# Spreading the reciprocal of `den` over the head dimension: from a round trip through DRAM to row-tiled TensorE products

## The chip, the cores and the metric

The kernel runs on one core of one Trainium2 chip. The metric is the device time of that core in microseconds (us); of several runs the median is taken.

## The reference, cut to what matters

The output is a sum of three parts, all from one layer-normalized input `xn` of 2048 tokens by 640 features: the input itself, a linear attention with 32 heads of 20 features (part A), and an update of the 8 tokens with the largest router score (part B).

```python
q, k, v = qkv[0], qkv[1], qkv[2]                     # 32 heads, Dh = 20
phi = lambda t: jnp.where(t > 0, t + 1, jnp.exp(t)) + 1e-6
pq, pk = phi(q), phi(k)
kv = jnp.einsum("bhsd,bhse->bhde", pk, v)
z = jnp.einsum("bhsd->bhd", pk)
num = jnp.einsum("bhqd,bhde->bhqe", pq, kv)
den = jnp.einsum("bhqd,bhd->bhq", pq, z)[..., None] + 1e-6
o = num / den
...                                                  # A = o @ wo
...                                                  # B = xn + update of 8 tokens
return x + _A_ref(xn, A_wqkv, A_wo) + _B_ref(xn, ...)
```

What the change touches is `num / den`. `den` has one value for each head and token; the kernel scales `pq` by `1/den` ahead of the last product, so each of these values is needed 20 times, once for each feature of its head.

## The kernel before, in words

Tokens lie in 16 tiles of 128. The order on each engine is the order in which the program issues its instructions; semaphores follow from which instruction reads and writes what.

1. A loop over the 16 tiles normalizes (VectorE `norm_dve`, with the reciprocal root by GpSimd `root_pool`, lines 186 and 187), transposes `xn` by DMA into `xnT` (`tr_dma`, SyncE, line 229), makes `k` (`k_half`, line 237) and `phi(k)` (`k_phi`), part of `q` (`q_mm`, line 274), and accumulates `xn` transposed times `pk` (`g1`, line 266). SyncE loads the weights of part B in pieces in between; the last weights (`wv`, `wo`, rest of `wu`, and `wd` by `load_wd`, line 131) are issued behind the loop.
2. A middle stage picks the 8 tokens, forms `kv` and multiplies it with `wo` into `Ms` (`kv_mm` line 617, `m_unit` line 634), runs the gated layer of part B (`gate_up`, line 717) and the rest of `q`. `pqT` holds `phi(q)` with features on partitions and tokens along the free axis.
3. `den_mm` (line 568) makes `den` with products tiled by columns: four chunks of tokens land on four groups of 32 partitions (32 heads each). `den_act` (lines 577 and 578) makes the reciprocal `rden` by Ln and Exp on ScalarE. This happens three times: for tokens 0 to 1023, 1024 to 1535 and 1536 to 2047.
4. `rden` has heads on partitions, and `pqT` has features on partitions. The spreading from one to the other goes through DRAM: `rden_out` or `rden_out_b` (line 595) writes each head's row 20 times into a DRAM tile, and `rden_in` or `rden_in_b` (line 601) reads it back into a part of `spare` with features on partitions. VectorE then multiplies `pqT` with it, 256 tokens at a time (`rden_mul`, line 605) and from tile 8 on 128 at a time (`rden_mul_b`, line 609). `sprb[0]` holds the spread values of tiles 8 to 11 and `sprb[1]` those of 12 to 15.
5. The last loop runs over the tiles, one `t` each: `o_mm` (line 782) makes ten products with `Ms` into two PSUM banks, banks 0 and 1 for even and 2 and 3 for odd `t`; `o_out` (line 791) adds `x` on VectorE and issues the store of the tile (line 796). At `t == 0` the loop holds the `down` products of part B (line 727), `den_mm` and `den_act` of the last 512 tokens, their way through DRAM (issues alternating between ScalarE and SyncE), and the scaling of the 8 updated rows `y8` on ScalarE (line 833), which GpSimd then adds by an indirect DMA to a DRAM copy of the late rows (`s_dram`, line 837). At `t == 5` ScalarE loads those rows back into `x_sb` (line 842). `rden_mul_b(t + 2)` stands behind `o_out(t)` for `t` from 6 to 13, so tile 12 is scaled behind `o_out(10)`. `o_last` (lines 803 to 821) does tile 15.

Of the kernel before, what the change touches and what calls it, by code (L numbers as in the profile page):

```python
# [8 lines left out]
P = 128  # L9
S = 2048  # L10
D = 640
H = 32
DH = D // H
F = 1536
T = S // P
KC = D // P
FC = F // P
# [12 lines left out]
BF16 = mybir.dt.bfloat16  # L30
# [4 lines left out]
ALU = mybir.AluOpType  # L35
# [3 lines left out]
def kernel(  # L39
# [12 lines left out]
    nc = tc.nc  # L52
    V, A, G, PE = nc.vector, nc.scalar, nc.gpsimd, nc.tensor
# [12 lines left out]
    def sb(name, shape, dtype=BF16):  # L66
        return sm.tile(shape, dtype, tag=name, name=name)

    ps = psum.tile([P, 8, 512], F32, tag="ps", name="ps")
    rd = tc.dram_tile([4, D, 256], BF16, name="rd")  # L70
    rdb = [tc.dram_tile([D, 512], BF16, name=f"rd{tb}") for tb in (2, 3)]
    s_dram = tc.dram_tile([S - NS, D], BF16, name="s_dram")

    x_sb = big.tile([P, T, D], BF16, tag="x_sb", name="x_sb")
# [9 lines left out]
    wu = big.tile([P, KC, F], BF16, tag="wu", name="wu")  # L84
# [3 lines left out]
    SP = nc.sync  # L88
# [20 lines left out]
    def kcw(w, src, lo, hi):  # L109
        SP.dma_start(w[:, lo:hi, :], src.rearrange("(kc p) n -> p kc n", p=P)[:, lo:hi, :])  # L110
# [19 lines left out]
    def load_wd(lo, hi):  # L130
        SP.dma_start(wd[:, lo:hi, :], B_w_down.rearrange("(fc p) n -> p fc n", p=P)[:, lo:hi, :])
# [42 lines left out]
    def stat(t, b):  # L174
        V.bn_stats(out=stats[:, t, b, :], in_=x_sb[:, t, b * HW : (b + 1) * HW])  # L175
        if b:
            V.bn_aggr(out=mv[:, t, :], in_=stats[:, t, :, :])  # L177

    def root_act(t):
        sl = slice(t, t + 1)  # L180
        A.activation(lg[:, sl], mv[:, t, 1:2], AF.Ln, bias=eps5[:])
        A.activation(rs[:, sl], lg[:, sl], AF.Exp, scale=-0.5)

    def root_pool(t, n=1):
        sl = slice(t, t + n)
        G.tensor_scalar_add(t2[:, sl], mv[:, sl, 1], EPS_BF16)  # L186
        G.tensor_tensor(out=rs[:, sl], in0=t2[:, sl], in1=mhalf[:, 0:n], op=ALU.pow)  # L187

    def shift(t, n):
        sl = slice(t, t + n)  # L190
        V.scalar_tensor_tensor(
            out=nm[:, sl], in0=mv[:, sl, 0], scalar=-1.0, in1=rs[:, sl], op0=ALU.mult, op1=ALU.mult
        )

    def norm_dve(t):
        V.tensor_scalar(  # L196
            out=xn[:, t, :], in0=x_sb[:, t, :], scalar1=mv[:, t, 0:1], scalar2=rs[:, t : t + 1],
            op0=ALU.subtract, op1=ALU.mult,
        )
# [28 lines left out]
    def tr_dma(t):  # L228
        nc.sync.dma_start_transpose(xnT[:, :, t * P : (t + 1) * P], xn[:, t, :])
# [3 lines left out]
    def k_half(t, b):  # L233
        b0 = K_BANK.get(t, 0)
        n = HW + (b if t else 0)
        for kc in range(KC):
            PE.matmul(  # L237
                ps[:, b0 + b, 0:n],
                lhsT=xnT[:, kc, t * P : (t + 1) * P],
                rhs=wk[:, kc, b * HW : b * HW + n],  # L240
                start=(kc == 0), stop=(kc == KC - 1),
            )
# [68 lines left out]
    def const_mask():  # L311
# [11 lines left out]
            G.tensor_copy(mask[:, b, :], m4[:, 4 * b : 4 * b + HB])  # L323
        return mask

    cst = {}

    def const_small():
# [120 lines left out]
    def adds(t, n):  # L449
        G.tensor_scalar_add(rs1[:, t : t + n], rs[:, t : t + n], 1.0)  # L450
        for i in range(t, t + n):
            add_s(i)
# [5 lines left out]
    for t in range(5, T):  # L458
        n = t + 4
        if 9 < n <= T:  # L460
            norm_dve(n - 1)
            tr_dma(n - 1)
            if pieces and n < T:
                kcw(*pieces.pop(0))
            shift(n - 1, 1)
        halves = (1, 0) if t == 5 else (0, 1)
        for b in halves:
            k_half(t, b)
        if n < T:
            if t == 5:  # L470
                stat(n, 0)
            stat(n, 1)
            root_pool(n)
        if n + 1 < T:
            stat(n + 1, 0)
        k_act(t, halves)
        if t == 5:
            root_act(8)
            norm_dve(8)
            tr_dma(8)  # L480
            kcw(*pieces.pop(0))
            k_phi(4)
            q_phi(2)
        if t in q_at:
            q_mm(q_at[t])
            q_act(q_at[t])
        if t > 5:
            g1(t - 4)
        k_phi(t)
        if t in q_at:  # L490
            q_phi(q_at[t])
        if t == 5:
            shift(0, 9)
        if t in add_at:
            adds(*add_at[t])

# [10 lines left out]
    load_cols(wv, 0, KC, 2 * D)  # L507
    load_wo()
    kcw(wu, B_w_up, 2, 3)
    kcw(wu, B_w_up, 3, KC)  # L510
    for i in range(0, FC, 4):
        load_wd(i, i + 4)
    PE.transpose(psb[0:T, 1, 0:P], r_all[:], ident[:])
    g1(T - 4)
    r_row = sb("r_row", [T, P], F32)
# [7 lines left out]
    for i, src in enumerate((cand, idxu)):  # L523
        V.tensor_tensor(
            out=candm[:, i, :, :], in0=src[:].unsqueeze(1).to_broadcast([T, T, C]), in1=sel_b,
# [7 lines left out]
        start=True, stop=True,  # L533
# [15 lines left out]
        out=junk[:, 0:C], in0=posf[:], scalar=1.0, in1=cst["sel8"][:], op0=ALU.mult, op1=ALU.mult,  # L549
# [3 lines left out]
        out=junk[:], in0=cst["iof"][:, 0:P], scalar=cols[:, 0:1], in1=allc[:, 1, :],  # L553
# [20 lines left out]
    def den_act(o, w, bank):  # L574
        ld = sm.tile([P, w], F32, tag="ld", name=f"ld{o}")
        rden = sb(f"rden{o}", [P, w])
        A.activation(ld[:], ps[:, bank, 0:w], AF.Ln, bias=cst["eps6"][:])
        A.activation(rden[:], ld[:], AF.Exp, scale=-1.0)
        return rden
# [14 lines left out]
    def rden_out_b(eng, i, rden, j):  # L594
        eng.dma_start(  # L595
            rdb[i][:, j * P : (j + 1) * P].rearrange("(h i) t -> h i t", i=DH),
            rden[32 * j : 32 * j + 32, :].unsqueeze(1).to_broadcast([32, DH, P]),
        )

    def rden_in_b(i):  # L600
        SP.dma_start(sprb[i], rdb[i][:, :].rearrange("(m p) t -> p m t", p=P))
# [5 lines left out]
    def rden_mul_b(t):  # L607
        sl = pqT[:, :, t * P : (t + 1) * P]
        V.tensor_tensor(  # L609
            out=sl, in0=sl, in1=sprb[t // 12][:, :, t % 4 * P : (t % 4 + 1) * P], op=ALU.mult  # L610
        )

    def kv_mm(bs, bank):
# [29 lines left out]
    for t in range(T):  # L643
        cols4 = pk[:, t, :].rearrange("p (m j f) -> p m j f", j=4, f=32)
        for j in range(4):
            PE.matmul(
                ps[32 * j : 32 * j + 32, 7, 0 : KC * 32].rearrange("p (m f) -> p m f", f=32),
                lhsT=cst["ones"][:], rhs=cols4[:, :, j, :],
                start=(t == 0), stop=(t == T - 1), tile_position=(0, 32 * j),
# [10 lines left out]
        out=junk[:, 0:C], in0=gv[:], scalar=1.0, in1=cst["sel8"][:], op0=ALU.mult, op1=ALU.mult,  # L660
# [8 lines left out]
        out=gate[:, 1:2], in0=gate[:, 0:1], scalar1=1e30, scalar2=1.0, op0=ALU.min, op1=ALU.add  # L669
# [6 lines left out]
        out=gate[:, 0:1], in0=cols[:, 1:2], scalar1=float(NS), scalar2=float(2 * S),  # L676
# [3 lines left out]
        out=gate[:, 1:2], in0=cols[:, 1:2], scalar=-float(NS), in1=gate[:, 0:1],  # L680
# [4 lines left out]
    for t in range(13, T):  # L685
        V.tensor_scalar(
            out=x_sb[:, t, :], in0=x_sb[:, t, :], scalar1=rs1[:, t : t + 1],
# [14 lines left out]
    sprb = [sp_rows(8, 12, 512), sp_rows(12, T, 512)]  # L702
# [21 lines left out]
    def down():  # L724
# [22 lines left out]
        out=eg[:, 1, :], in0=eg[:, 0, :], scalar1=1e30, scalar2=1.0, op0=ALU.min, op1=ALU.add  # L747
# [40 lines left out]
    def o_out(t):  # L788
        b0 = 2 * (t % 2)
        o_t = evk.tile([P, 2, HW], BF16, tag=("ek", "rk")[t % 2], name=f"o{t}")  # L790
        V.tensor_tensor(  # L791
            out=o_t[:], in0=ps[:, b0 : b0 + 2, 0:HW],
            in1=x_sb[:, t, :].rearrange("p (b f) -> p b f", b=2), op=ALU.add,
        )
        eng = nc.sync if t % 2 == 0 and t > 2 else nc.scalar
        eng.dma_start(out_v[:, t, :], o_t[:].rearrange("p b f -> p (b f)"))

    def o_last(t):
# [24 lines left out]
    for t in range(T - 1):  # L823
        o_mm(t)
        if t == 0:
            down()
            den_mm(1536, P, 6)
            rden3 = den_act(1536, P, 6)
            for j in range(4):
                rden_out_b((A, SP)[j % 2], 1, rden3, j)  # L830
            rden_in_b(1)
            for i in range(4):
                A.activation(  # L833
                    y8[:, i * QW : (i + 1) * QW], ps[32 * i : 32 * i + C, 5 + 2 * (i % 2), 0:QW],
                    AF.Identity, scale=gate[32 * i : 32 * i + C, 2:3],
                )
            G.indirect_dma_start(  # L837
                s_dram[:, :], bass.IndirectOffsetOnAxis(ap=idx_i[0:C, 1:2], axis=0), y8[:], None,
                bounds_check=S - NS - 1, oob_is_err=False, compute_op=ALU.add,
            )  # L840
        if t == 5:
            A.dma_start(x_sb[:, TS:T, :], s_dram[:, :].rearrange("(t p) d -> p t d", p=P))
        o_out(t)
        if t < 2:
            rden_mul(t + 2)
        if 6 <= t < 14:
            rden_mul_b(t + 2)
        if t == TS - 1:
            G.indirect_dma_start(
                out[0, 0:NS, :], bass.IndirectOffsetOnAxis(ap=idx_i[0:C, 0:1], axis=0), y8[:], None,  # L850
                bounds_check=NS - 1, oob_is_err=False, compute_op=ALU.add,
            )
# [29 lines left out]
```

## Time and profile before

| | |
|---|---|
| median of 3 runs | 113.27 us (113.08 to 116.18) |
| the profiled execution | 112.75 us, of which the span of the profile is 111.0 us |
| TensorE products busy | 104.3 us (94% of the span) |
| VectorE busy | 81.2 us (73%) |
| ScalarE busy | 58.9 us (53%) |
| GpSimd busy | 39.2 us (35%) |
| DMA | 23.65 MB, mean 213 GB/s |
| granted TensorE clock | 1.00 |

The profile shows one execution. PE is TensorE's products, PEld its weight loads, DVE VectorE, ACT ScalarE, POOL GpSimd, SP SyncE; a `q` behind the name means the engine's queue, issuing a DMA or waiting for a semaphore. A share of busy time is a mean over stages with different limits; the waits and the chain of work that ended last tell which wait counts.

### The profile page before, as it was taken

The page shows a single profiled execution, that of the slowest core. Times are in us where ns is not written, and L with a number is a line of the kernel's source. Part 1 is how long each engine was busy: PE and PEld are TensorE (multiplying, and loading weights), DVE is VectorE, ACT ScalarE, POOL GpSimd, SP SyncE. Part 2 cuts the span into 40 slices and gives each one's busy share as a digit, 9 for nine tenths or more (in the row PEclk, how much of TensorE's full clock was granted, in tenths as well). Part 3 has the DMA queues.
Part 4 walks back from the last instruction along what each step waited for, and adds up shares of the span by engine and source line. Part 5 has one row for each costly group of instructions (what it writes and reads, how often), then busy time and mean ns, then how long its engine had stood idle before and what let it go on. Part 6 is the DMA issues. An engine that isn't in the chain of part 4 may idle for free.

```text
span 111.0 us, 2501 instructions
## 1 busy us (share of the span) xinstructions
PE 104.3 (94%) x897; PEld 61.8 (56%) x906; DVE 81.2 (73%) x186; ACT 58.9 (53%) x155; POOL 39.2 (35%) x86
## 2 busy tenths in 40 slices
PE   5899999999999999999999999999999999994990
PEld 2256645555555555564447788534457776662660
DVE  1798997789999996544349745696799766884780
ACT  1449996797877666555058352788894400000000
POOL 6903563211344448899993420000000050000040
PEclk9999999999999999999999999999999999999999
DMA  3999435792679998999999949369868199999243
GB/s 81 324 328 297 152 68 101 197 240 59 183 189 203 210 177 206 224 220 302 235 388 365 304 110 287 98 173 302 292 91 151 51 344 254 242 359 386 89 124 118
DMA packets 31655, 23.65 MB, mean 213 GB/s; under 512 B 14194, under 2 KB 30362, under 8 KB 31642
## 3 DMA queue, kind: packets, MB, share of 16 engines
q1 hardware_dynamic: 25168, 18.97, 64.3%
q10 hardware_dynamic: 6410, 4.51, 13.2%
q8 instruction: 7, 0.11, 0.5%
q14 instruction: 6, 0.05, 0.2%
q0 software_dynamic: 64, 0.01, 0.2%
HBM read 15.44 MB, written 6.08 MB: 194 GB/s over the span
## 4 chain that ended last, share of the span: by engine, by line
PE 73%; DMA 14%; ACT 3%; issue 3%; DVE 2%; ACTq 2%; SPq 0%
PE ps L274 19%; PE ps L237 19%; PE ps L266 16%; PE ps L782 5%; DMA spare<-rd 5%; DMA out_dram<-o 4%; PE ps L502 4%; DMA rd<-rden 3%; DMA x_sb<-in_A_x_dram 2%; PE ps L617 2%; PE ps L634 2%; PE ps L717 2%; PE ps L215 1%; PE ps L808 1%; ACTq L595 1%
## 5 line engine op out<-in xcount | busy, mean ns | idle before, releaser
L237 PE MATMUL ps<-wk,xnT 128*128 128x320 bf16 (+1 forms) x160 | 25.0, 300 | 0.1
L274 PE MATMUL ps<-xnT,wq 128*128 128x512 bf16 x93 | 22.9, 379 | 0.6 <-issue 0.3
L782 PE MATMUL ps<-late,pqT 128*128 128x320 bf16 x150 | 21.6, 299 | 1.4 <-DVE pqT L609 1.4
L237 PEld LDWEIGHTS <-xnT 128*128 128x128 bf16 x160 | 15.1, 98 | 8.7 <-ACT xnT L221 0.9
L266 PE MATMUL ps<-pk,xn 128*128 128x512 bf16 x78 | 19.5, 379 | 0.1
L251 ACT ACTIVATE ek<-ps 128x320 bf16<-128x320 f32 x32 | 14.8, 463 | 8.1 <-PE ps L237 8.1
L782 PEld LDWEIGHTS <-pqT 128*128 128x128 bf16 x150 | 14.1, 98 | 8.7 <-DVE pqT L609 3.1
L283 ACT ACTIVATE eq<-ps 128x512 bf16<-128x512 f32 x20 | 11.9, 597 | 9.0 <-PE ps L274 9.0
L175 DVE BATCH_NORM_STATS2 stats<-x_sb 128x6 f32<-128x320 bf16 x32 | 14.8, 474 | 2.3 <-DMA x_sb<-in_A_x_dram 2.3
L290 DVE SCALAR_TENSOR_TENSOR pqT<-eq,rq 128x512 bf16<-128x512 bf16 x20 | 13.7, 685 | 3.7 <-ACT rq L284 3.7
L259 DVE SCALAR_TENSOR_TENSOR pk<-ek,rk 128x640 bf16<-128x640 bf16 x16 | 13.0, 813 | 4.2 <-ACT rk L252 4.2
L791 DVE TENSOR_TENSOR o<-ps,x_sb 128x640 bf16<-128x640 f32 x15 | 12.3, 823 | 4.7 <-PE ps L782 3.5
L274 PEld LDWEIGHTS <-wq 128*128 128x128 bf16 x100 | 9.3, 98 | 10.7 <-issue 0.7
L252 ACT ACTIVATE rk<-ps 128x320 bf16<-128x320 f32 x32 | 14.8, 463 | 0.0
L207 POOL TENSOR_SCALAR x_sb<-x_sb,rs,nm 128x640 bf16<-128x640 bf16 x13 | 13.8, 1068 | 0.6
L266 PEld LDWEIGHTS <-xn 128*128 128x128 bf16 x80 | 7.7, 98 | 8.1
L284 ACT ACTIVATE rq<-ps 128x512 bf16<-128x512 f32 x20 | 11.9, 593 | 0.0
L186 POOL TENSOR_SCALAR t<-mv 128x1 bf16<-128x1 f32 x12 | 3.8, 316 | 21.7 <-DVE mv L177 21.4
L818 ACT CAST o<-ps 128x160 bf16<-128x160 f32 x1 | 0.3, 292 | 19.1 <-PE ps L808 19.1
L187 POOL TENSOR_TENSOR rs<-t,mhalf 128x1 f32<-128x1 bf16 x12 | 10.0, 834 | 1.0
L837 POOL DMA_INDIRECT s_dram<-y,idx_i x1 | 1.6, 1594 | 23.2 <-ACT y L833 23.2
L196 DVE TENSOR_SCALAR xn<-x_sb,mv,rs 128x640 bf16<-128x640 bf16 x16 | 7.2, 450 | 3.3 <-POOL rs L187 2.8
(123 smaller groups left out, 98.6 us busy)
## 6 DMA issues: line engine op xcount, KB each, us to landing
spare<-rd SPq DMA_DIRECT2D x4, 640.0 KB, 5.4
wg<-in_B_w_gate_dram SPq DMA_DIRECT2D x5, 384.0 KB, 3.4
wd<-in_B_w_down_dram SPq DMA_DIRECT2D x3, 640.0 KB, 13.5
out_dram<-o ACTq DMA_DIRECT2D x9, 160.0 KB, 4.0
rd<-rden ACTq DMA_DIRECT2D x1, 1280.0 KB
wu<-in_B_w_up_dram SPq DMA_DIRECT2D x3, 384.0 KB, 3.5
wo<-in_A_wo_dram SPq DMA_DIRECT2D x2, 500.0 KB, 7.7
x_sb<-in_A_x_dram SPq DMA_DIRECT2D x3, 320.0 KB, 5.8
```

What stands on the lines that cost most here:

```text
L175: V.bn_stats(out=stats[:, t, b, :], in_=x_sb[:, t, b * HW : (b + 1) * HW])
L207: G.tensor_scalar(out=x_sb[:, t, :], in0=x_sb[:, t, :], scalar1=rs1[:, sl], scalar2=nm[:, sl], op0=ALU.mult, op1=ALU.add,)
L237: PE.matmul(ps[:, b0 + b, 0:n], lhsT=xnT[:, kc, t * P : (t + 1) * P], rhs=wk[:, kc, b * HW : b * HW + n], start=(kc == 0), stop=(kc == KC ...
L251: A.activation(e[:, b, :], ps[:, b0 + b, 0:HW], AF.Exp)
L252: A.activation(r[:, b, :], ps[:, b0 + b, 0:HW], AF.Relu)
L259: V.scalar_tensor_tensor(out=pk[:, t, :].rearrange("p (b f) -> p b f", b=2), in0=e[:], scalar=1.0, in1=r[:], op0=ALU.min, op1=ALU.add,)
L266: PE.matmul(ps[:, 2 + c, :], lhsT=xn[:, t, c * P : (c + 1) * P], rhs=pk[:, t, 0:512], start=(t == 0), stop=(t == T - 1),)
L274: PE.matmul(ps[:, bank, :], lhsT=wq[:, kc, m * P : (m + 1) * P], rhs=xnT[:, kc, tb * 512 : (tb + 1) * 512], start=(kc == 0), stop=(kc == K ...
L283: A.activation(e[:], ps[:, bank, :], AF.Exp)
L290: V.scalar_tensor_tensor(out=pqT[:, m, tb * 512 : (tb + 1) * 512], in0=e[:], scalar=1.0, in1=r[:], op0=ALU.min, op1=ALU.add,)
L782: PE.matmul(ps[:, b0 + b, 0:HW], lhsT=pqT[:, kc, t * P : (t + 1) * P], rhs=Ms[:, kc, b * HW : (b + 1) * HW], start=(kc == 0), stop=(kc == ...
L791: V.tensor_tensor(out=o_t[:], in0=ps[:, b0 : b0 + 2, 0:HW], in1=x_sb[:, t, :].rearrange("p (b f) -> p b f", b=2), op=ALU.add,)
```

## The change

The spread for the last 512 tokens no longer goes through DRAM. A constant `grep` holds a 1 where a feature belongs to a head (32 partitions by 640), made by GpSimd in three instructions within the tile loop (`t` of 6 to 8) and copied by three DMAs to the other three groups of 32 partitions. `spread_mm` multiplies, for each of the five blocks of 128 features and each of the four chunks of 128 tokens, 32 rows of `grep` with 32 rows of `rden`, in row tiles of TensorE, into PSUM banks 4 to 7. `spread_copy` copies the result by ScalarE into `sprb[1]`. Four blocks of features are done at `t == 3`, the fifth at `t == 5`. `den_act` of these tokens now stands behind the four `y8` instructions. Besides, all even stores of the output are issued by SyncE (before: those of `t` above 2), one load of `wu` is split into two, and `wd` is loaded in four parts instead of three.

```diff
-    rdb = [tc.dram_tile([D, 512], BF16, name=f"rd{tb}") for tb in (2, 3)]
+    rdb = [tc.dram_tile([D, 512], BF16, name="rd2")]
...
+    grep = sb("grep", [P, D])
+
+    def const_grep(i):
+        g = grep[0:32, :]
+        if i == 0:
+            G.memset(g, 1.0)
+        else:
+            base, sgn = ((0, 1), (DH - 1, -1))[i - 1]
+            G.affine_select(
+                out=g, in_=g, compare_op=ALU.is_ge, fill=0.0, base=base,
+                pattern=[[sgn, D]], channel_multiplier=-sgn * DH,
+            )
+
+    def copy_grep():
+        for j in range(1, 4):
+            SP.dma_start(grep[32 * j : 32 * j + 32, :], grep[0:32, :])
...
+        if 6 <= t < 9:
+            const_grep(t - 6)
...
-    kcw(wu, B_w_up, 3, KC)
-    for i in range(0, FC, 4):
-        load_wd(i, i + 4)
+    kcw(wu, B_w_up, 3, 4)
+    kcw(wu, B_w_up, 4, KC)
+    for i in range(0, FC, 3):
+        load_wd(i, i + 3)
+    copy_grep()
...
+    def spread_mm(rden, ms):
+        for i, m in enumerate(ms):
+            for j in range(4):
+                PE.matmul(
+                    ps[:, 4 + j, i * P : (i + 1) * P],
+                    lhsT=grep[32 * j : 32 * j + 32, m * P : (m + 1) * P],
+                    rhs=rden[32 * j : 32 * j + 32, :],
+                    start=(i == 0), stop=True, tile_position=(32 * j, 0), skip_group_check=True,
+                )
+
+    def spread_copy(ms, j, n):
+        w = len(ms)
+        dst = sprb[1][:, ms[0] : ms[0] + w, j * P : (j + n) * P]
+        A.copy(
+            dst.rearrange("p m (j f) -> p j m f", j=n),
+            ps[:, 4 + j : 4 + j + n, 0 : w * P].rearrange("p j (m f) -> p j m f", m=w),
+        )
...
-        eng = nc.sync if t % 2 == 0 and t > 2 else nc.scalar
+        eng = nc.sync if t % 2 == 0 else nc.scalar
...
             den_mm(1536, P, 6)
-            rden3 = den_act(1536, P, 6)
-            for j in range(4):
-                rden_out_b((A, SP)[j % 2], 1, rden3, j)
-            rden_in_b(1)
             for i in range(4):
                 A.activation(y8[...], ...)
             G.indirect_dma_start(s_dram[:, :], ...)
+            rden3 = den_act(1536, P, 6)
+        if t == 3:
+            spread_mm(rden3, range(0, 4))
+            for j in (0, 2):
+                spread_copy(range(0, 4), j, 2)
         if t == 5:
+            spread_mm(rden3, range(4, 5))
+            spread_copy(range(4, 5), 0, 4)
             A.dma_start(x_sb[:, TS:T, :], s_dram[:, :].rearrange("(t p) d -> p t d", p=P))
```

## The prediction

> **What bounds the kernel now.** I read the busy time of the engines first, then the chain of work that ended last, then the waits, and last the timeline of each engine around the one stall.
>
> ```profile
> PE 104.3 (94%) x897; PEld 61.8 (56%) x906; DVE 81.2 (73%) x186; ACT 58.9 (53%) x155; POOL 39.2 (35%) x86
> PE 73%; DMA 14%; ACT 3%; issue 3%; DVE 2%; ACTq 2%; SPq 0%
> ```
>
> TensorE (PE) is busy nearly all the time. DMA holds 14% of the chain, and in order of time most of that share sits in one place:
>
> ```profile
> 85.71 0.32 ACT rden L578
> 88.33 4.73 DMA out_dram<-o
> 93.08 3.19 DMA rd<-rden
> 96.33 5.34 DMA spare<-rd
> 101.69 0.50 DVE pqT L609
> ```
>
> The values `rden` are there at 86.03 and their spread form at 101.7: ScalarE's half of the writes flies until about 92, then SyncE's half, then the read of 5.34. The waits of SyncE's queue tell why the halves do not overlap: it waits for a write in flight.
>
> ```profile
> SPq L595 <- DMA rd<-rden: 5.6, 1, 5.6
> ```
>
> Most of these 15 us is hidden: PE works on tiles 1 to 11 meanwhile and stalls once, for 1.43 us. The timeline shows the stall in place, VectorE first, then PE's weight loads and products (idle time before each in brackets):
>
> ```profile
> 98.00 0.82 DVE L791 TENSOR_TENSOR o<-ps,x_sb 128x640 bf16<-128x640 f32 x1 [0.29 <-issue]
> 98.74 0.48 DVE L609 TENSOR_TENSOR pqT<-pqT,spare 128x640 bf16<-128x640 bf16 x1
> 99.39 0.82 DVE L791 TENSOR_TENSOR o<-ps,x_sb 128x640 bf16<-128x640 f32 x1 [0.17 <-issue]
> 101.69 0.49 DVE L609 TENSOR_TENSOR pqT<-pqT,spare 128x640 bf16<-128x640 bf16 x1 [1.48 <-DMA spare<-rd]
> 94.85 1.20 PEld L782 LDWEIGHTS <-pqT 128*128 128x128 bf16 x10 [0.20 <-DVE pqT L609]
> 99.27 1.20 PEld L782 LDWEIGHTS <-pqT 128*128 128x128 bf16 x10 [0.31 <-DVE pqT L609]
> 102.23 2.56 PEld L782 LDWEIGHTS <-pqT 128*128 128x128 bf16 x20 [1.76 <-DVE pqT L609]
> 85.14 15.67 PE L782 MATMUL ps<-late,pqT 128*128 128x320 bf16 x110
> 102.24 4.44 PE L782 MATMUL ps<-late,pqT 128*128 128x320 bf16 x30 [1.43 <-DVE pqT L609]
> ```
>
> **What is removed.** Without the wait, the scaling of tile 12 follows `o_out(10)` as the scaling before it followed `o_out(9)`: 0.74 behind its start (98.00 to 98.74), at 99.39 + 0.74 = 100.13. The loads come 0.53 later (98.74 to 99.27), at 100.66 instead of 102.23: 1.57 us. PE's own idle time says 1.43. I take 1.45; more cannot go, since PE is busy on both sides of the stall. The five issues that go (four writes of 160 KB and one read of 640 KB) were on no path but this one.
>
> **What is added on PE.** Twenty products of 32 rows, 128 weight columns and 128 streamed columns. The trace has no product tiled by rows; the nearest rows:
>
> ```profile
> 82.47 1.52 PE L782 MATMUL ps<-late,pqT 128*128 128x320 bf16 x10
> 83.92 1.01 PE L727 MATMUL ps<-wd,late 128*32 128x160 bf16 x48
> 84.76 0.45 PE L568 MATMUL ps<-pqT,zm 128*32 128x128 bf16 x20
> 60.24 2.40 PE L502 MATMUL ps<-pk,xn 128*128 128x128 bf16 x40
> 66.55 2.07 PE L617 MATMUL ps<-GT,wv 128*80 128x64 bf16 x50
> 63.45 1.03 PE L274 MATMUL ps<-xnT,wq 128*128 128x512 bf16 x4 [0.16 <-issue]
> ```
>
> Low end: `den_mm` (L568) has four tiles side by side too, and the same 128 streamed columns; its twenty take from 84.76 to 85.14, 0.38 us. High end: if the four tiles do not overlap, streaming or loading sets the pace. The 40 full products of L502 take 2.40 us, 60 ns each: 1.2 us for twenty. The 50 of L617 stream only 64 columns but load 80, and take 2.07 us, 41 ns each; if loading sets that, 128 columns take 66 ns: 1.32 us for twenty. I take 0.5, near L568, which shares what decides (four tiles at once), with a little for four times the weight columns.
>
> There are two blocks, so four changes between tiled and full products. From `o_mm(0)` to `down` the start moves by 1.45 us for ten products, of which a tile without scaling takes 1.39 (below): 0.06 for a change. The row at 63.45 shows 0.16 idle behind a tiled block. Bounds 0 and 0.64 for four; I take 0.25, by the first row. Sum on PE: 0.75, between 0.38 and 1.96.
>
> [...]
>
> When does PE reach these products, and is the operand there?
>
> ```profile
> 85.31 0.37 ACT L577 ACTIVATE ld<-ps,eps 128x128 f32<-128x128 f32 x1 [1.56 <-issue]
> 88.70 0.39 ACT L833 ACTIVATE y<-ps,gate 8x160 bf16<-8x160 f32 x1
> L651 ACT CAST GT<-ps 128x1024 bf16<-128x1024 f32 x1 | 1.0, 1020 | 0.0
> L654 ACT CAST GT<-ps 128x512 bf16<-128x512 f32 x1 | 0.6, 632 | 0.0
> ```
>
> Seven tiles, 1 to 7, lie between 85.14 (products) and 94.85 (loads of tile 8): 1.39 us a tile. So `o_mm(3)` ends near 89.3. ScalarE is idle until 85.3; the four `y8` can take from 85.0 to 86.6, then `ld` and `rden` (0.37 and 0.32) to 87.3. That is 2 us early and frees banks 5 to 7 as well. With that cover gone, the 0.7 us of `den_act`, moved behind `y8`, would stand on PE's path.
>
> **What is added on ScalarE.** Two copies of 128 by 1024 (L651, 1.02 each) and one of 128 by 512 (L654, 0.63), 2.7 us on an engine that computes nothing between 89.1 and 108. The first two run from about 89.8 to 91.9. The fifth block of products writes the same banks; PE is there two tiles later, at 92.6. That is 0.7 us of cover, and each microsecond beyond it costs PE one. Queued behind the copies are the stores of tiles 3 and 5, for which nobody waits soon, and the load of the late rows:
>
> ```profile
> 93.63 0.39 ACTq L842 DMA_DIRECT2D x_sb<-s_dram  x1
> x_sb<-s_dram ACTq DMA_DIRECT2D x1, 800.0 KB, 5.4
> s_dram<-y,idx_i POOLq DMA_INDIRECT x1, 4.1
> ```
>
> `y8` is ready at 86.6 instead of 89.1, so the indirect add (4.1) lands near 90.8 and no longer sets the load's issue; the third copy does, at about 93.4. The rows land 5.4 later, near 98.8, and `o_out(11)` wants them near 101.4 (102.1 of the stalled run less the gain). VectorE wants the copies at 100.8, and they are done at 93.3. Cost zero, with 2.5 and 7 us of cover; beyond it, one for one.
>
> **Stores.** Tiles 0 and 2 move to SyncE:
>
> ```profile
> 92.15 1.48 SPq L595 DMA_DIRECT2D rd<-rden  x2
> 96.79 11.11 SPq L796 DMA_DIRECT2D out_dram<-o  x6
> ```
>
> It held back its even stores until 96.79 behind the writes and the read that now go. Nothing of this is on the chain: zero.
>
> **GpSimd, and the loads.** The memset and two selects that make `grep` fall into GpSimd's gaps in the tile loop:
>
> ```profile
> 1.14 0.29 POOL masks.py:199 TENSOR_SCALAR_AFFINE_SELECT ident<-ident 128x128 bf16<-128x128 bf16 x1
> 1.69 0.77 POOL L304 TENSOR_SCALAR_AFFINE_SELECT headg<-headg 128x160 bf16<-128x160 bf16 x2
> 35.06 0.22 POOL L186 TENSOR_SCALAR t<-mv 128x1 bf16<-128x1 f32 x1 [1.34 <-DVE mv L177]
> 45.21 1.21 SPq L229 DMA_TRANSPOSE xnT<-xn  x1
> xnT<-xn SPq DMA_TRANSPOSE x12, 3.1
> 49.58 1.37 PE ps L237 x10
> SPq L589 <- DMA rd<-rden: 16.2, 1, 16.2
> ```
>
> A select of 640 elements costs at least 0.29 and, scaled by size, at most 1.54 (four times half of 0.77). `ident` has one pattern dimension as here and part of its 0.29 is fixed, so I take 0.8; the gap is 1.34. An overrun would delay `rs`, the normalization and the transposes. The last tile has 1.27 us in hand: its transpose is issued at 45.21, lands 3.1 later and is used at 49.58. Cost zero; beyond this, one for one. SyncE's five more issues stand ahead of L589, where it waits 16.2 us anyway: zero.
>
> **Sum.** Against the profiled execution: 112.75 - 1.45 + 0.75 = 112.05 us, a span of 110.3. The median shown, 113.27, lies 0.5 above that execution and the fastest run 0.33, so I forecast 112.4 for a median; its own range is 111.5 (1.57 gained, 0.38 paid) to 113.0. About 2% (2.3 us) is what a measurement of this kernel can tell from no change; this is 0.8%.
>
> **Rivals.** *Loads or streaming set the pace:* 1.32 for the products and 0.4 for the changes, 113.0 for the execution and 113.4 for a median. For it: L617, and the lack of any row-tiled product in the trace. Against: L568 and L727 overlap well.
>
> *Slower: each product of another row tile waits until the one before has left the array.*
>
> ```profile
> L568 PE MATMUL ps<-pqT,zm 128*32 128x128 bf16 x40 | 0.9, 220 | 0.0
> ```
>
> Such a product lasts 220 ns by itself; twenty in a row are 4.4 us instead of 0.5, and 112.4 + 3.9 = 116.3. It loses time from 60 ns a product on ((1.45 - 0.25) / 20). For it: another bank and another row group each time, a form not seen here. Against: column tiles show no such wait.
>
> *GpSimd overruns:* two selects of 1.54 at twice the time are 3.1 each, 3.5 too long together, less 1.27 in hand: 112.4 + 2.2 = 114.6. Against: only part of VectorE's work in the loop could double them.
>
> *The stall stays*, with another releaser (late rows, or copies held up in ScalarE's queue), and PE pays 0.75: 113.27 + 0.75 = 114.0. Against: 2.5 and 7 us of cover.
>
> *Faster by more:* products for nothing, 112.75 - 1.57 = 111.2; and scaled tiles, at 1.47 us (94.85 to 99.27 for three) against 1.39, gain 0.6 over eight if that was due to DMA traffic: 110.6. Against: the pace is the dependence on VectorE, as the bracketed waits show.
>
> **How the numbers follow.** Forecast 0.50, loads or streaming 0.13, drained products 0.16, GpSimd 0.06, stall stays 0.08, faster by more 0.07. The range of 111.3 to 114.8 leaves out the drained products and some of the last: under 2 in 10. Slower by over 2%: the drained products and parts of the two near 114, 0.20. Faster by over 2%: most of the last, 0.06. Within 2%: 0.74.
>
> **What would show it.** Right: L609 waits for no DMA, PE's idle 1.43 is gone, tile 12 is scaled 0.74 behind the start of `o_out(10)`, the spread products take 0.8 with their gaps, the first two copies 1.0 each and end ahead of the fifth block, transposes stand where they stood. Wrong: 60 ns or more from one spread product to the next, PE waiting for ScalarE at `t` of 3 or 5, VectorE waiting longer for `rs`, or a stall of 1 us at tiles 11 to 13.

## The result, and the profile after

The changed kernel takes 111.9 us (median of 5 runs, 111.72 to 112.03) against 113.27 (median of 5). The ratio is 0.9887, with a 95% interval from 0.9871 to 0.9903: 1.1% less time, clear of the noise and within the 2% that the prediction called "same". The forecast was 112.4, and 112.05 for the profiled execution, which took 111.9 with a span of 110.2 (110.3 forecast). Medians in this text are over all runs, while a ratio leaves out the most disturbed ones and is taken against the kernel before as it ran beside that experiment, so experiments on the changed kernel are compared with it by their times.

The page of the changed kernel, busy time and the chain that ended last:

```profile
PE 105.5 (96%) x926; PEld 61.9 (56%) x926; DVE 83.9 (76%) x186; ACT 61.4 (56%) x158; POOL 41.3 (38%) x89
PE 89%; ACT 3%; DMA 2%; DVE 2%; issue 1%; ACTq 0%
```

DMA's share of the chain fell from 14% to 2%, PE's rose from 73% to 89%: the way through DRAM has left the chain, and PE holds it from the first tile to the last.

The timeline of the last loop, by engine: ScalarE's `y8`, `rden` and first copies; the two blocks of spread products and the full products behind each; VectorE at tile 12; the loads of tiles 8 and 12.

```profile
84.99 1.58 ACT L870 ACTIVATE y<-ps,gate 8x160 bf16<-8x160 f32 x4 [1.22 <-PE ps L768]
87.00 0.31 ACT L600 ACTIVATE rden<-ld 128x128 bf16<-128x128 f32 x1
89.34 0.40 PE L639 MATMUL ps<-rden,grep 32*128 32x128 bf16 x16
89.67 2.89 PE L823 MATMUL ps<-late,pqT 128*128 128x320 bf16 x20
89.78 1.01 ACT L649 CAST spare<-ps 128x1024 bf16<-128x1024 f32 x1 [2.47 <-PE ps L639]
90.68 1.02 ACT L649 CAST spare<-ps 128x1024 bf16<-128x1024 f32 x1
92.50 0.23 PE L639 MATMUL ps<-rden,grep 32*128 32x128 bf16 x4
92.66 13.16 PE L823 MATMUL ps<-late,pqT 128*128 128x320 bf16 x90
92.92 0.38 ACTq L886 DMA_DIRECT2D x_sb<-s_dram  x1
95.58 1.20 PEld L823 LDWEIGHTS <-pqT 128*128 128x128 bf16 x10 [0.36 <-DVE pqT L631]
100.11 0.82 DVE L832 TENSOR_TENSOR o<-ps,x_sb 128x640 bf16<-128x640 f32 x1 [0.32 <-issue]
100.85 0.48 DVE L631 TENSOR_TENSOR pqT<-pqT,spare 128x640 bf16<-128x640 bf16 x1
101.39 1.20 PEld L823 LDWEIGHTS <-pqT 128*128 128x128 bf16 x10 [0.34 <-DVE pqT L631]
106.76 0.51 PE L849 MATMUL ps<-late,pqT 128*128 128x160 bf16 x5
```

Tile 12 is scaled 0.74 behind the start of `o_out(10)`, with no wait for a DMA, and PE's 90 products run in one piece where 1.43 us stood idle. The sixteen products of the first block end in full products 0.33 after they start, the four of the second 0.16. The two copies are done at 91.70 (90.68 + 1.02), 0.8 ahead of the block that reuses their banks.

Where the time went: the loads of tile 12 begin at 101.39 instead of 102.23, 0.84 earlier, and the last products of the kernel at 106.76 instead of 107.61. The way from the loads of tile 8 to those of tile 12 took 7.38 us (94.85 to 102.23) and takes 5.81 (95.58 to 101.39): 1.57 us, the price of the wait. Of these, 0.50 pays for the two blocks (0.33 and 0.17 in the chain), and 0.23 is lost between tiles 4 and 8, whose loads start 0.73 later. Ahead of this nothing was won or lost: the products of tile 1 start at 85.16 instead of 85.14, so neither the split loads nor the making of the constant shows in the time.

One thing moved that was to stay. In the tile loop, GpSimd's memset and first select, each with VectorE's normalization beside it, and the last transpose and its products:

```profile
30.72 0.62 POOL L332 MEMSET grep<- 32x640 bf16 x1
30.86 0.67 DVE L196 TENSOR_SCALAR xn<-x_sb,mv,rs 128x640 bf16<-128x640 bf16 x1
33.71 0.78 POOL L335 TENSOR_SCALAR_AFFINE_SELECT grep<-grep 32x640 bf16<-32x640 bf16 x1
33.83 0.84 DVE L196 TENSOR_SCALAR xn<-x_sb,mv,rs 128x640 bf16<-128x640 bf16 x1
46.03 1.21 SPq L229 DMA_TRANSPOSE xnT<-xn  x1
49.43 1.53 PE L237 MATMUL ps<-wk,xnT 128*128 128x320 bf16 x10
```

In the kernel before, the second of these normalizations:

```profile
33.82 0.44 DVE L196 TENSOR_SCALAR xn<-x_sb,mv,rs 128x640 bf16<-128x640 bf16 x1
```

It took 0.44 in this place before; beside the select it takes 0.84, and beside the memset 0.67. The last transpose comes 0.82 later than before, and PE still starts the last tile's products where it did (49.42 before).

### The profile page after: what moved, and what is told of

Read it like the earlier page. It is cut to its first block, busy times and chain, and to the rows that moved or that the text cites. A ratio compares the mean times of both kernels' runs of the same rounds, so it can differ in the third digit from the quotient of the medians.

```text
span 110.2 us, 2558 instructions
## 1 busy us (share of the span) xinstructions
PE 105.5 (96%) x926; PEld 61.9 (56%) x926; DVE 83.9 (76%) x186; ACT 61.4 (56%) x158; POOL 41.3 (38%) x89
## 4 chain that ended last, share of the span: by engine, by line
PE 89%; ACT 3%; DMA 2%; DVE 2%; issue 1%; ACTq 0%
PE ps L274 20%; PE ps L823 19%; PE ps L237 18%; PE ps L266 16%; PE ps L522 4%; DMA x_sb<-in_A_x_dram 2%; PE ps L658 2%; PE ps L675 2%; PE ps L758 2%; PE ps L849 1%; PE ps L215 1%; PE ps L590 1%; PE ps L687 1%; DVE xn L196 1%; PE ps L768 1%; DVE stats L175 1%
## 5 line engine op out<-in xcount | busy, mean ns | idle before, releaser
L274 PE MATMUL ps<-xnT,wq 128*128 128x512 bf16 x100 | 23.7, 379 | 0.0
L290 DVE SCALAR_TENSOR_TENSOR pqT<-eq,rq 128x512 bf16<-128x512 bf16 x20 | 14.2, 709 | 3.5 <-ACT rq L284 3.4
L175 DVE BATCH_NORM_STATS2 stats<-x_sb 128x6 f32<-128x320 bf16 x32 | 14.7, 473 | 2.1 <-DMA x_sb<-in_A_x_dram 1.9
L259 DVE SCALAR_TENSOR_TENSOR pk<-ek,rk 128x640 bf16<-128x640 bf16 x16 | 14.0, 874 | 2.4 <-ACT rk L252 2.3
L207 POOL TENSOR_SCALAR x_sb<-x_sb,rs,nm 128x640 bf16<-128x640 bf16 x13 | 12.6, 982 | 0.6
L196 DVE TENSOR_SCALAR xn<-x_sb,mv,rs 128x640 bf16<-128x640 bf16 x16 | 8.2, 515 | 3.3 <-POOL rs L187 2.8
```

Of the source, the lines that this page charges most:

```text
L207: G.tensor_scalar(out=x_sb[:, t, :], in0=x_sb[:, t, :], scalar1=rs1[:, sl], scalar2=nm[:, sl], op0=ALU.mult, op1=ALU.add,)
L259: V.scalar_tensor_tensor(out=pk[:, t, :].rearrange("p (b f) -> p b f", b=2), in0=e[:], scalar=1.0, in1=r[:], op0=ALU.min, op1=ALU.add,)
L274: PE.matmul(ps[:, bank, :], lhsT=wq[:, kc, m * P : (m + 1) * P], rhs=xnT[:, kc, tb * 512 : (tb + 1) * 512], start=(kc == 0), stop=(kc == K ...
L290: V.scalar_tensor_tensor(out=pqT[:, m, tb * 512 : (tb + 1) * 512], in0=e[:], scalar=1.0, in1=r[:], op0=ALU.min, op1=ALU.add,)
```

## The experiments

My theory: the gain is the stall that the way through DRAM left at tile 12, less what the products cost PE. The rivals: it comes from the stores and lighter queues; the DRAM way only needed another order; the products are hidden and cost nothing.

**The stores alone, on the kernel before** (`e1_stores_only`).

```diff
-        eng = nc.sync if t % 2 == 0 and t > 2 else nc.scalar
+        eng = nc.sync if t % 2 == 0 else nc.scalar
```

> The kernel before, with only the store change: tiles 0 and 2 stored by SyncE. My theory (the gain is the removed stall and nothing from the stores): SyncE issues these two stores behind its writes and the read of the spread values, at about 96.5, and since an even tile's buffer comes back four even tiles later, o_out(8) must wait for the store of tile 0, until about 99.5 instead of 96.5. That takes the place of the stall at tile 12 and is longer: 114 to 115.5 us against 113.2. The rival (the lighter queues are the gain): 112 to 113.

Measured: 120.29 us, ratio 1.0623 [1.057, 1.0676]. The waits of this run, and two stretches of it (length, busy time of each engine, granted clock, DMA share, GB/s):

```profile
DVE o L791 <- DMA out_dram<-o: 8.0, 1, 8.0
PE ps L782 <- DVE pqT L609: 7.7, 1, 7.7
104.00:108.00 4.00, 2.54 (x10) 1.46 (x11) 2.36 (x4) 0.00 (x0) 0.00 (x0) 0.50 0.39 136
108.00:112.00 4.00, 4.00 (x19) 2.27 (x17) 2.15 (x4) 0.00 (x0) 0.08 (x1) 0.57 0.12 41
```

The mechanism was as expected: `o_out(8)` waits for the store of tile 0, which SyncE issued behind the spread's read. Its size was not: the wait is 8 us instead of 3, since the read was issued at 98.47 and not at 96.3, and the store behind it (98.94) landed only at 104.2. Behind PE's stall of 7.7 us the granted clock is 0.50 and 0.57 (the column ahead of the DMA share), and a tile takes about twice as long for some 6 us (3.08 and 2.67 us from one `o_out` to the next, against 1.39). The store change is no gain by itself; it is free once the spread has left SyncE's queue.

**The stores put back, on the changed kernel** (`e5_stores_back`): the same line, the other way.

> The changed kernel with the stores of tiles 0 and 2 back on ScalarE's queue. My theory (the stores give nothing by themselves once SyncE has no writes and reads of the spread in front of them): 111.8 to 112.0, within 0.1 of the changed kernel. The rival (ScalarE needs to be free of them for the copies): the second block of products waits for the copies, 112.3 or more.

Measured: 111.79 us (111.75 to 112.1), ratio 0.9833 [0.9762, 0.9904]. Within 0.1 of the changed kernel: the stores give nothing. This rival is out.

**The spread products twice, on the changed kernel** (`e3_products_twice`).

```diff
             spread_mm(rden3, range(0, 4))
+            spread_mm(rden3, range(0, 4))
...
             spread_mm(rden3, range(4, 5))
+            spread_mm(rden3, range(4, 5))
```

> The changed kernel with both blocks of spread products issued twice (forty instead of twenty). My theory: the products lie on the path that sets the end, 21 ns each, so the time grows by 0.4 to 0.5: 112.3 to 112.4. The rival (the products are hidden, since the scaled tiles wait for VectorE anyway): 111.9, within 0.1.

Measured: 112.19 us (112.01 to 112.38), ratio 0.993 [0.9907, 0.9953]: 0.3 more. The chain of the changed kernel has these two pieces for the products,

```profile
89.41 0.33 PE ps L639 x16
92.56 0.17 PE ps L639 x4
```

and that of this run these:

```profile
89.25 0.56 PE ps L639 x32
92.63 0.22 PE ps L639 x8
```

Twenty more products cost 0.23 + 0.05 = 0.28 us, 14 ns each, and all of it reaches the end: the last products begin 21.89 us behind those of tile 1 (85.00 to 106.89) instead of 21.60 (85.16 to 106.76). They are on the path, and cheaper than I took them. What is left of the 0.50 is 0.22 for four changes between tiled and full products, 0.055 each. What the 0.055 pay for is not shown.

**All DRAM writes by SyncE** (`e2_sp_writes`), **all by ScalarE** (`e8_act_writes`), both on the kernel before: does the way through DRAM only need its halves to fly together?

```diff
-                rden_out_b((A, SP)[j % 2], 1, rden3, j)
+                rden_out_b(SP, 1, rden3, j)        # e2; in e8: rden_out_b(A, 1, rden3, j)
```

> The kernel before, with all four DRAM writes of the last 512 tokens issued by SyncE, so that none waits for a write of the other queue. My theory (the stall came from the halves flying one after the other): issues end near 89, writes land near 93, the read lands near 98.5, ahead of the 100.1 at which VectorE wants it, the stall of 1.43 goes without any product added: 111.3 to 111.9 for a median, ratio to before 0.983 to 0.988. The rival (the way through DRAM is too long in any order, TensorE is needed): a stall of 0.7 us or more stays, 112.6 to 113.3.

> The kernel before with all four DRAM writes of the last 512 tokens issued by ScalarE, ahead of its stores, so that no write waits for another queue, nor (as with all on SyncE) for a landing semaphore that a later store holds. My theory (the stall came from the order of the halves, not from the flight itself): writes issued by 88.8, landed near 93.5, read landed near 98.5, no stall at tile 12: 111.3 to 111.9 for a median. Rival one (the way through DRAM is too long in any order): a stall of 0.7 or more stays, 112.6 to 113.3. Rival two (ScalarE is held 1.4 us longer and the late rows come too late for o_out(11)): a stall moves to the late rows, 112.3 to 113.

Measured: 118.93 us for SyncE, ratio 1.0519 [1.0479, 1.056]; 114.75 for ScalarE, ratio 1.0093 [1.0049, 1.0137]. Both expectations of mine missed, in `e2` the rival's time as well; in `e8` the second rival had the place of the stall right, but not its time (112.3 to 113). The waits in `e2`:

```profile
SPq L595 <- DMA out_dram<-o: 5.2, 2, 3.4
SPq L595 <- DMA x_sb<-s_dram: 4.1, 1, 4.1
DVE pqT L609 <- DMA spare<-rd: 5.4, 1, 5.4
```

and two neighbouring pieces of its chain:

```profile
92.58 5.04 DMA x_sb<-s_dram
97.64 3.01 DMA rd<-rden
```

SyncE's writes wait for stores (5.2 us) and for the late rows (4.1), which ScalarE issues and with whose data they have nothing to do: the write issued at 97.64 follows by 0.02 the landing of the late rows' load, issued at 92.58. The trace of the kernel before shows such a wait with its semaphore: the DMA issues of SyncE and ScalarE name eight landing semaphores between them, handed round, and SyncE's write issued at 93.08 has that of a store which ScalarE issued at 88.33 and which landed at 93.06. In `e8`, VectorE's wait and row at tile 12, and the stretch behind it:

```profile
DVE o L791 <- DMA x_sb<-s_dram: 2.8, 1, 2.8
100.21 0.48 DVE L609 TENSOR_TENSOR pqT<-pqT,spare 128x640 bf16<-128x640 bf16 x1
104.00:108.00 4.00, 3.26 (x16) 2.05 (x17) 3.04 (x6) 0.00 (x0) 1.40 (x1) 0.71 0.27 88
```

The spread values are in time here: tile 12 is scaled at 100.21 without a wait. But `y8` stood behind four issues, the late rows came too late for `o_out(11)`, and a wait of 2.8 us took the place of that of 1.48.

**ScalarE's writes behind `y8`** (`e11_act_writes_y8_first`), the order of the changed kernel with the way through DRAM:

```diff
-            rden3 = den_act(1536, P, 6)
-            for j in range(4):
-                rden_out_b((A, SP)[j % 2], 1, rden3, j)
-            rden_in_b(1)
             for i in range(4):
                 A.activation(y8[...], ...)
             G.indirect_dma_start(s_dram[:, :], ...)
+            rden3 = den_act(1536, P, 6)
+            for j in range(4):
+                rden_out_b(A, 1, rden3, j)
+            rden_in_b(1)
```

> The kernel before with y8 and the indirect add first, then den_act, and all four DRAM writes issued by ScalarE: the order of the changed kernel, but the way through DRAM. My theory (only the order of queues and instructions made the way through DRAM late): writes issued from 87.3 to 90.4, landed near 95, read landed near 100, late rows as in the changed kernel: stall at tile 12 of 0.5 or less, 111.4 to 112.2. The rival (the way through DRAM is too long and too uncertain even in the best order): a stall of 1 us or more at tile 12, 112.6 or more.

Measured: 114.48 us, ratio 1.0048 [0.9997, 1.01]. The rival's case. The late rows are fine, but the read is issued only at 94.86, and its 7.55 us are longer than the 5.34 of the kernel before; stores and the late rows are in flight beside it, but what makes it longer is not shown. The chain and the wait:

```profile
94.86 7.55 DMA spare<-rd
DVE pqT L609 <- DMA spare<-rd: 2.2, 1, 2.2
```

So in three orders the wait stayed or moved: 5.4 and 2.2 us at tile 12, or 2.8 at the late rows. That no order of it could work is not shown; the TensorE route needs none.

**Copies three times** (`e10_copies_thrice`), on the changed kernel, to test the cover of the fifth block:

```diff
-            for j in (0, 2):
+            for j in (0, 2) * 3:
                 spread_copy(range(0, 4), j, 2)
```

> The changed kernel with ScalarE's two copies of the first block done three times each, in the same place. My theory (TensorE is back for the fifth block 0.8 us after the copies end, and beyond that each microsecond costs one): four copies more are 3.6 us, TensorE stands still for 2.8, and the time is 114.7 if it goes on at full pace. What the stalls of 2.5 to 7.7 us in the other runs showed (a granted clock of 0.5 to 0.7 for some microseconds behind them) would add 1 to 2.5 us: 115.7 to 117.2. The rival (TensorE does not wait there, or the wait is swallowed by the pace of VectorE): 111.9 to 112.5.

Measured: 116.31 us, from 114.67 to 117.1, ratio 1.0178 [1.004, 1.0317]. The profiled execution took 114.67 and shows PE waiting inside the fifth block:

```profile
94.34 0.23 PE L639 MATMUL ps<-rden,grep 32*128 32x128 bf16 x2 [1.94 <-ACT spare L649]
95.26 0.23 PE L639 MATMUL ps<-rden,grep 32*128 32x128 bf16 x2 [0.69 <-ACT spare L649]
```

The two runs at 114.67 had a granted clock of 1.000 and land on the one-for-one price (114.7). The four runs at 116.3 to 117.1 had 0.985, in the range that I expected if the clock falls behind the stall; of these no profile was taken, so that the stall set it off is not shown.

**Scaling three tiles ahead** (`e4_scale_ahead`), on the changed kernel:

```diff
-        if 6 <= t < 14:
-            rden_mul_b(t + 2)
+        if 5 <= t < 13:
+            rden_mul_b(t + 3)
```

> The changed kernel with each tile from 8 on scaled three tiles ahead of its products instead of two. My theory (scaled tiles take 1.45 us instead of 1.39 because each waits for VectorE's scaling one tile earlier): weight loads no longer wait for L631, the gain is 0.4 to 0.6, 111.3 to 111.5. The rival (the slower pace is DMA traffic or VectorE's own limit): 111.8 to 112.0.

Measured: 111.13 us (110.98 to 111.67), ratio 0.9847 [0.9811, 0.9883]: 0.8 us less than the changed kernel, more than I expected. PE's products and loads in one unbroken run each:

```profile
92.52 12.40 PE L823 MATMUL ps<-late,pqT 128*128 128x320 bf16 x90
92.52 12.07 PEld L823 LDWEIGHTS <-pqT 128*128 128x128 bf16 x90
```

Ninety products take 12.40 instead of 13.16, with the same DMA traffic. The slower pace of the scaled tiles was the dependence on VectorE. For tiles 12 to 15 it is the spread by TensorE that makes this edit possible: their values are there at 93.4, and through DRAM they came at 101.7. For tiles 8 to 11, whose values still come through DRAM, it might have helped the kernel before too; that was not tried.

**More selects, and the constant made late** (`e6_selects_more`, `e7_grep_late`), on the changed kernel:

```diff
         if 6 <= t < 9:
             const_grep(t - 6)
+        if 9 <= t < 11:                            # e6
+            const_grep(t - 8)
```

> The changed kernel with the two selects of GpSimd done a second time, at t of 9 and 10 of the tile loop (the values stay the same). My theory (each select holds up VectorE's normalization beside it by 0.4 us, the last transposes came 0.8 later in the changed kernel than before, and only about 0.4 of cover is left): the transposes of the last tiles come 0.8 later again, products of L237 wait for them, 112.2 to 112.6. The rival (the delay is hidden behind other slack): 111.8 to 112.0.

> The changed kernel with the constant made and copied late, behind the picking of the 8 tokens (GpSimd idle from 66 us), instead of within the tile loop. My theory (what GpSimd takes from VectorE in the tile loop is hidden by the cover of 1.27): time as the changed kernel, 111.8 to 112.0, with VectorE's normalizations back at 0.45 and the last transposes 0.8 earlier. The rival (the later normalizations cost time somewhere): 111.0 to 111.5. If the late selects instead hold up VectorE where TensorE waits for it: 112.3 or more.

In `e7` the three instructions and the copies stand behind `load_s`, at 65.8 us. Measured: 112.34 us with two selects more, ratio 0.9886 [0.981, 0.9961]; 111.77 with the constant made late, ratio 0.984 [0.9765, 0.9915]. In `e6` PE waits for the last transpose; the line of normalizations of `e7` against the page of the changed kernel follows:

```profile
49.89 1.54 PE L237 MATMUL ps<-wk,xnT 128*128 128x320 bf16 x10 [0.25 <-DMA xnT<-xn]
```

```profile
L196 DVE TENSOR_SCALAR xn<-x_sb,mv,rs 128x640 bf16<-128x640 bf16 x16 | 7.2, 447 | 3.4 <-POOL rs L187 2.8
```

```profile
L196 DVE TENSOR_SCALAR xn<-x_sb,mv,rs 128x640 bf16<-128x640 bf16 x16 | 8.2, 515 | 3.3 <-POOL rs L187 2.8
```

Two selects more bring the last tile's products 0.46 later (49.43 to 49.89) and the kernel 0.44. Made late, the constant holds up nothing, and the time stays within 0.2 of the changed kernel. So what GpSimd takes from VectorE was hidden, with about 0.5 of the 1.27 left (in `e6` the last transpose is issued 0.98 later, at 47.01, and 0.46 of it costs).

**The two edits together** (`e9_ahead_late`): `e4` and `e7`.

> The changed kernel with both edits that did not hurt: tiles from 8 on scaled three tiles ahead, and the constant made behind the picking of the tokens. My theory (the first is worth 0.8 us, the second moves work that is hidden either way): 111.0 to 111.3, as with the scaling alone. The rival (they add up to more, since the late transposes cost a little in the tile loop): below 110.9.

Measured: 111.1 us (110.96 to 111.27), ratio 0.9769 [0.9706, 0.9831]. No more than `e4` by itself, as the theory had it. With `e4` it is the fastest version here; both beat the changed kernel by 0.8 us.

## Why the prediction was right

*The stall.* It went, as the bracketed wait had said: tile 12 follows `o_out(10)` by 0.74, and the whole 1.57 of the loads came back. The sum took 1.45, with the reason that no more could go because PE is busy on both sides of the stall; that reason was wrong, by 0.12. `e5` shows that nothing of the gain is the stores'.

*The products.* 0.50 instead of 0.75. The changes between modes were sized right (0.22 for 0.25). The products were the mis-sized term: 0.28 instead of 0.5, since I added something for four times the weight columns, and there was nothing to add: 14 ns each is under the 19 of `den_mm` with 32 weight columns. The loads, by duration (ns, shortest, median and longest):

```profile
L639 PEld LDWEIGHTS <-grep x20: 90/92/94, 89.3 to 92.5; 32*128 32x128 bf16 x20
```

A single load lasts 92 ns in the profile, and 14 ns lie between one product with its load and the next, so the loads overlap; twenty one after the other would be 1.8 us. Neither the rival of loads or streaming nor that of drained products came true.

*A cost I left out.* The 0.23 between tiles 4 and 8. Two tiles between the blocks take 2.83 us instead of 2.77; the two behind the second block take 2.92, and there tile 8's loads wait for VectorE (0.36 idle). In `e4`, with scaling one tile earlier, no such wait is left and the 2.83 stay, so about 0.15 of the 0.23 is that dependence. That the sum came out so close is in part luck: 0.25 less for the products and 0.12 more for the wait against 0.23 left out, 112.05 forecast for the execution and 111.9 measured.

*ScalarE.* `rden` at 87.31 (87.3 forecast), copies done at 91.70 (91.9), PE back at 92.50 (92.6), late rows issued at 92.92 (93.4). The cover of 0.7 was 0.8, and `e10` shows the price beyond it: one for one, while the clock stayed at 1.00.

*GpSimd.* A select takes 0.78, as I took it (0.8), and the cost was zero. But the reason I gave was not the whole: I looked whether the selects fit into GpSimd's gap, not what runs on VectorE in that gap. The sign "transposes stand where they stood" failed: the last came 0.82 later. With a cover of 0.4 instead of 1.27, this would have cost about 0.4, as two selects more did in `e6`. In the rows the normalization that starts 0.12 behind the select ends 0.18 behind its end, 0.40 longer than before, and the one beside the memset ends 0.19 behind that one's end; what makes them longer is not shown. The doubling that the GpSimd rival feared exists in the kernel before: `rs` took 0.57 where VectorE was at its statistics (L175), and 1.11 where it made `pk` and `pqT` (L259, then L290):

```profile
24.83 0.57 POOL L187 TENSOR_TENSOR rs<-t,mhalf 128x1 f32<-128x1 bf16 x1
24.80 0.49 DVE L175 BATCH_NORM_STATS2 stats<-x_sb 128x6 f32<-128x320 bf16 x1 [0.36 <-DMA x_sb<-in_A_x_dram]
32.61 1.11 POOL L187 TENSOR_TENSOR rs<-t,mhalf 128x1 f32<-128x1 bf16 x1
32.49 0.81 DVE L259 SCALAR_TENSOR_TENSOR pk<-ek,rk 128x640 bf16<-128x640 bf16 x1
```

The selects took 0.78 both times, and behind each GpSimd still waited 0.99 for VectorE's `mv`: no gap was overrun.

*The median.* I set it 0.35 above the profiled execution, as in the kernel before; after the change both are 111.9. This is most of the 0.5 by which the forecast was too high (0.35; the other 0.15 is that of the sum). Why the kernel before lies higher in most runs than in the profiled one is not shown; its own way through DRAM is a likely place, since that read took 5.34 us in its profile and 4.8 and 7.6 in those of `e2` and `e11`.

## What to carry to other kernels

Of a transfer that was almost in time only the end was paid for here (a stall of 1.43 us on PE, of the 15 from `rden` to its spread form), so credit a change with the stall and not with the transfer; then look at what the earlier arrival allows, which here (scaling one tile further ahead) was worth another 0.8 us. Ask of an instruction added in a gap what the neighbour engine does in that gap, not only whether the gap is long enough (the normalization beside a select took 0.84 us instead of 0.44). And a reordering of DMA issues is no small edit: four of them here (`e1`, `e2`, `e8`, `e11`) turned a stall of 1.43 us on PE into one of 2.15 to 7.7 in their profiles, through queue order, waits for the landing of other DMAs and a longer flight.

## What the runs showed of the hardware that I had not expected

In some runs a stall came with more lost time than its length, as in four of `e10` (116.3 to 117.1 us, against 114.67 at one for one). Behind PE's stall of 1.43 us in the kernel before the granted clock stayed 1.00 in the profiled run, and so it did behind 2.15 us in `e11`; behind 2.46 us (`e8`, profiled in a run of 116.17) it was 0.71 over 4 us; behind 7.7 us (`e1`) it was 0.50 and 0.57; and behind 5.4 us (`e2`) 0.59 and 0.55. The stalls of `e11` and `e8`, and the clock behind those of `e11` and `e2`:

```profile
102.97 4.44 PE L782 MATMUL ps<-late,pqT 128*128 128x320 bf16 x30 [2.15 <-DVE pqT L609]
104.74 4.57 PE L782 MATMUL ps<-late,pqT 128*128 128x320 bf16 x20 [2.46 <-DVE pqT L609]
104.00:108.00 4.00, 3.98 (x31) 2.64 (x30) 3.05 (x6) 0.00 (x0) 1.35 (x1) 1.00 0.42 145
104.00:108.00 4.00, 1.89 (x8) 1.08 (x9) 1.62 (x3) 0.00 (x0) 0.00 (x0) 0.59 0.78 279
108.00:112.00 4.00, 4.00 (x18) 2.35 (x17) 1.56 (x3) 0.00 (x0) 1.35 (x1) 0.55 0.19 58
```

With 2.6 us in two pieces the profiled run of `e10` kept 1.00. Over whole runs, the granted clock was 0.985 or less in 4 of the 6 runs of `e10`, in 5 of 12 each of `e8` and `e11`, in all 10 of `e1` and `e2`, and in 25 of the 47 of the kernel before beside the experiments; in the 42 of the changed kernel and its versions without such a stall (`e3` to `e7`, `e9`) it was never below 0.996. So in these runs the lower clock comes with the stall; that the stall sets it off is argued from one profile of each version, not shown.
